# Two attention and mixer layers on one core: where the softmax's small operations stand between VectorE's long products

## The chip, the core and the metric

The kernel runs on one core of a Trainium2 chip. The engines named below are TensorE (PE, matrix products), VectorE (DVE), ScalarE (ACT), GpSimd (POOL) and SyncE (SP, which issues the DMA transfers). The metric is the device time of one execution in microseconds. Before the change it is 1139.48 us, the median of three runs (1139.33 to 1139.99).

## The reference

The input x has 2048 rows of 640 numbers. Two times over, an attention layer and a mixer MLP are added to it:

```
x = x + A(layernorm(x));  x = x + B(layernorm(x));  x = x + A(layernorm(x));  x = x + B(layernorm(x))

A: q, k, v = x @ wqkv            # 640 x 1920, 32 heads of 20 numbers
   row s looks at the rows s, s-2, ..., s-14 (8 keys, those before row 0 masked)
   o = softmax(q.k * 20**-0.5) @ v;   return o @ wo
B: return gelu(x @ w1 + b1) @ w2 + b2      # 640 -> 1536 -> 640
```

Layer norm takes away a row's mean and divides by the root of its variance plus 1e-5. All is float32; the kernel splits each operand of a large product into a float16 and the rest in float16, and adds three products.

## The kernel before

The rows are cut into four units of 512; a unit is four tiles of 128 rows. With two layers there are eight blocks, n = 0 to 7. A block goes through these steps.

- Layer norm "a" (L579 on). A tile's statistics come either from DVE (`FAST` tiles: `bn_stats`, `bn_aggr`, L597 to L599) or from ACT (mean L607, squares L611, variance L621). GpSimd raises variance plus epsilon to the power -0.5: this is "the root", L624 (L602 for a `FAST` tile). ACT then forms a factor (L629), the tile is normalised (ACT L649 or L682, DVE L645), split (ACT L655 or L715 for the high half, L657 or L717 on DVE or POOL for the rest) and transposed by DMA (L659, L720, L725).
- The projection to q, k and v on PE: L913 with evictions L933 in blocks 0 to 3; in blocks 4 to 7 by seven products instead of eight (L841, evictions L850 and L859, sums L873; the layer norm's rows are added up in L688 to L695). The result goes out to memory and is fetched back shifted (L965).
- Attention in four groups of eight heads, 32 groups G in all, on DVE: product q*k (L1007, 128x5120), sum over 20 (L1012), mask (L1016, in the units that begin at row 0), maximum (L1019), difference (L1020), exp on ACT (L1022), sum (L1024), reciprocal (L1025), product (L1026), then the product with v (L1028, 128x5120), and sums over the eight keys (L1033 twice, L1036). ACT L1041 and L1044 (DVE or POOL) split the result; DMA transposes it (L1053).
- The output projection on PE (L1065), in a bank that ACT fills with x first (L1077) and evicts (L1082).
- Layer norm "b", and the MLP: first product L1132 on PE, gelu L1138 and its high half L1141 on ACT, the rest L1143 on DVE or POOL, second product L1153. The weights are split from float32 (ACT L542, L543, DVE or POOL L544), spilled and loaded again (L1125). The MLPs of the last two blocks are computed together at the end (L1293 on).

No loop sets the order in which an engine does its work. Every operation is handed to the class `Plan` (L86) with its engine, its duration, a priority (lower goes first) and its inputs. `Plan.run` plays a clock for each engine, takes the operation that can start first, and writes down the order; the program is emitted in that order, and each engine issues its own instructions in it, one behind the other. So a table such as `ROWS_AT` (the priorities of the layer norms by block) moves instructions on all engines. `wait` is how long DVE is kept for an urgent operation (`PATIENCE` for those below -200), `hold` a time that an operation on DVE is kept back after it could run, for the benefit of POOL. An operation of the kind `either` is done on DVE, or on POOL if it fits beside a reduction L1012.

Operations on DVE that read two operands in the on-chip memory carry `pair=True` (their kinds stand in `PAIRS`). The plan assumes that a root cannot begin while one of them runs. It keeps these stretches in a list `shut`; a root that falls in one is planned at its end. Two such operations that follow each other are one stretch, unless the second is of a kind in `LETS`, or the first was the product with v. This rule is arithmetic in the plan alone: the chip is told of no dependency from a root to DVE's operations.

## Time and profile before

| | |
|---|---|
| profiled execution | 1139.51 us, span 1137.7 us |
| PE busy | 1121.7 us, 99% |
| DVE busy | 1050.8 us, 92%; 25.00 of the 25 us from 600 on, 17.27 of the next 25 |
| ACT busy | 665.4 us, 58%, 20 table loads each at L1022 and L1138 |
| POOL busy | 163.8 us, 14%, of these 69.1 in 31 roots L624 |
| idle of PE ahead of L1065 | 5.6 us in 3 waits, the longest 4.4 us |

A row of the timeline reads: start and duration in us, engine, line, operation, what it writes and reads, how many instructions in a row, and in brackets how long the engine stood idle before it and what ended that. A row of the page's list of groups has after the bar the busy time, the mean of one in ns, and the idle time in front of the group with its releasers. PEld is PE's loading of weights, which runs beside the products. PE's granted clock is given as a share of the full clock. An engine's operation can be recorded as beginning a little before the one ahead of it ends.

### The profile page before, as it was taken

The page shows a single profiled execution, that of the slowest core. Times are in us where ns is not written, and L with a number is a line of the kernel's source. Part 1 is how long each engine was busy: PE and PEld are TensorE (multiplying, and loading weights), DVE is VectorE, ACT ScalarE, POOL GpSimd, SP SyncE. Part 2 cuts the span into 40 slices and gives each one's busy share as a digit, 9 for nine tenths or more (in the row PEclk, how much of TensorE's full clock was granted, in tenths as well). Part 3 has the DMA queues.
Part 4 walks back from the last instruction along what each step waited for, and adds up shares of the span by engine and source line. Part 5 has one row for each costly group of instructions (what it writes and reads, how often), then busy time and mean ns, then how long its engine had stood idle before and what let it go on. Part 6 is the DMA issues. An engine that isn't in the chain of part 4 may idle for free. (4 is left out here: it accounts for less than half of the span.)

```text
span 1137.7 us, 17017 instructions
## 1 busy us (share of the span) xinstructions
PE 1121.7 (99%) x6536; PEld 603.1 (53%) x6536; DVE 1050.8 (92%) x894; ACT 665.4 (58%) x1226; POOL 163.8 (14%) x111
## 2 busy tenths in 40 slices
PE   9999999999999999999999899999999999999998
PEld 6444464445545455455544454456445555654476
DVE  7999999999999999999999799999989998668972
ACT  6468345657856455655745576369744752858630
POOL 1116001201022011210013431003300200000000
PEclk9999999999999999999999999999999999999999
DMA  9999675889898797687786679859698656695201
GB/s 316 299 331 263 204 202 166 296 266 299 258 315 252 199 296 216 204 215 187 288 223 218 141 190 229 307 188 226 150 349 239 184 189 167 175 258 157 68 24 70
DMA packets 262605, 250.91 MB, mean 221 GB/s; under 512 B 154412, under 2 KB 219260, under 8 KB 262524
## 3 DMA queue, kind: packets, MB, share of 16 engines
q1 hardware_dynamic: 262524, 249.83, 75.5%
q8 instruction: 51, 0.84, 0.3%
q14 instruction: 30, 0.25, 0.1%
HBM read 161.49 MB, written 52.64 MB: 188 GB/s over the span
## 5 line engine op out<-in xcount | busy, mean ns | idle before, releaser
L1153 PE MATMUL acc<-c,act 128*128 128x512 f16 (+1 forms) x1728 | 250.9, 299 | 0.5 <-ACT acc L1113 0.3
L1132 PE MATMUL ps<-yT,c 128*128 128x512 f16 x1080 | 246.3, 381 | 3.1 <-issue 2.6
L913 PE MATMUL ps<-wq,yT 128*128 128x480 f16 (+1 forms) x990 | 196.6, 360 | 0.4 <-ACT wq L509 0.4
L1153 PEld LDWEIGHTS <-act 128*128 128x128 f16 x1728 | 136.7, 98 | 112.1 <-issue 0.9
L1028 DVE TENSOR_TENSOR pr<-sm,v 128x5120 f32<-128x5120 f32 x32 | 176.5, 5516 | 0.4
L1007 DVE TENSOR_TENSOR pr<-qk 128x5120 f32<-128x5120 f32 x32 | 175.4, 5481 | 0.2
L1012 DVE TENSOR_REDUCE sm<-pr 128x256 f32<-128x5120 f32 x32 | 175.3, 5478 | 0.2
L1132 PEld LDWEIGHTS <-c 128*128 128x128 f16 x1080 | 103.4, 98 | 126.0 <-issue 5.1
L913 PEld LDWEIGHTS <-yT 128*128 128x128 f16 x990 | 95.4, 98 | 98.5 <-issue 0.5
L1065 PE MATMUL ps<-wo,yT 128*128 128x320 f16 x960 | 134.7, 302 | 5.6 <-ACT ps L1077 5.6
L1033 DVE TENSOR_TENSOR pr<-pr 128x2560 f32<-128x2560 f32 x64 | 137.5, 2148 | 0.1
L624 POOL TENSOR_TENSOR ln<-ln,half 128x2 f32<-128x2 f32 (+1 forms) x31 | 69.1, 2229 | 356.0 <-ACT ln L621 355.9
L1065 PEld LDWEIGHTS <-yT 128*128 128x128 f16 x960 | 94.7, 99 | 45.1 <-issue 5.8
L841 PE MATMUL ps<-wq,yT 128*128 128x480 f16 x528 | 112.2, 366 | 1.1 <-ACT ev L850 1.1
L1138 ACT ACTIVATE act<-ps,b 128x512 f32<-128x512 f32 x72 | 49.2, 683 | 84.0 <-PE ps L1132 83.5
L850 ACT ACTIVATE ev<-ps 128x480 f32<-128x480 f32 x96 | 53.6, 567 | 75.4 <-PE ps L841 72.8
L841 PEld LDWEIGHTS <-yT 128*128 128x128 f16 x528 | 51.1, 98 | 54.9 <-issue 1.5
L841 PE MATMUL ps<-wq 128*128 128x480 f16 x336 | 72.0, 366 | 0.0
L933 ACT ACTIVATE ev<-ps 128x480 f32<-128x480 f32 x64 | 36.1, 566 | 58.6 <-PE ps L913 58.1
L1044 POOL TENSOR_TENSOR ohl<-w,ohl 128x640 f16<-128x640 f32 x18 | 25.2, 1402 | 243.7 <-DVE sm L1024 61.5
L1141 ACT ACTIVATE act<-act 128x512 f16<-128x512 f32 x72 | 44.8, 623 | 22.3 <-PE acc L1153 22.0
L1143 DVE TENSOR_TENSOR act<-act 128x512 f16<-128x512 f32 x64 | 43.6, 685 | 10.6 <-ACT act L1141 10.6
(225 smaller groups left out, 1309.7 us busy)
## 6 DMA issues: line engine op xcount, KB each, us to landing
c<-mw SPq DMA_DIRECT2D x126, 320.0 KB, 3.8
spill<-ev SPq DMA_DIRECT2D x64, 480.0 KB, 4.1
qk<-spill SPq DMA_DIRECT2D x32, 880.0 KB, 5.6
v<-spill SPq DMA_DIRECT2D x32, 880.0 KB, 4.9
qk<-spill SPq DMA_DIRECT2D x32, 320.0 KB, 3.2
c<-in_B_w_dram SPq DMA_DIRECT2D x24, 320.0 KB, 5.2
mw<-c SPq DMA_DIRECT2D x24, 320.0 KB, 4.9
pr<-in_B_w_dram SPq DMA_DIRECT2D x24, 320.0 KB, 4.5
```

What stands on the lines that cost most here:

```text
L624: pool(0.5, prio, lambda t0=t0, t1=t1: nc.gpsimd.tensor_tensor(col(2)[:, t0:t1], col(2)[:, t0:t1], half[:, t0:t1], op=OP.pow), need=[("vr" ...
L841: nc.tensor.matmul(ps, r(x_, j), w[:, j, y_], start=start and i == 0, stop=i == len(todo) - 1, skip_group_check=True)
L850: act(C, -400 + n, lambda: nc.scalar.activation(to(), tile_of(*bank)[:, :C].rearrange("p (a c) -> p a c", a=3), AF.Copy, scale=1.0 / WS), ...
L913: nc.tensor.matmul(ps, transposed(yk)[:, a * KD + k, t * P:(t + 1) * P], wq[:, g, k, b, i0 * GC:i1 * GC], start=first and j == 0, stop=las ...
L1007: nc.vector.tensor_mul(pr.rearrange("p w t c -> p w (t c)"), w[:, HALO + m:HALO + 2 * m].rearrange("p t c -> p (t c)")[:, None, :].to_broa ...
L1012: dve(E, G - 0.7, lambda: nc.vector.tensor_reduce(by_key(), heads(), axis=AX.X, op=OP.add), need=[("qk", G)], give=[("lg", G)], use=[*pk, sk])
L1028: dve(E, G - 0.85, lambda: nc.vector.tensor_mul(heads(), by_key()[:, :, :, None].to_broadcast([P, W, m * GH, DH]), windows(tile_of(*vw), [ ...
L1033: dve(m * w * GC, G - 0.9, lambda w=w: nc.vector.tensor_add(pr[:, 0:w], pr[:, 0:w], pr[:, w:2 * w]), need=[last], give=[("ad", G, w)], use=vk)
L1065: nc.tensor.matmul(tile_of(*pk)[:, :D // 2], transposed(yk)[:, a * KD + k, t * P:(t + 1) * P], wo[:, b, k, c * D // 2:(c + 1) * D // 2], s ...
L1132: nc.tensor.matmul(tile_of(*pk)[:, :nt], tile_of(*ck)[:, a, k * P:(k + 1) * P], transposed(yk)[:, c * KD + k, t0 * P:t1 * P], start=i == 0 ...
L1138: act(nt, -430, lambda pk=pk, h32=h32, e=e: nc.scalar.activation(tile_of(*h32)[:, :nt], tile_of(*pk)[:, :nt], AF.Gelu_apprx_tanh, bias=b1[ ...
L1153: nc.tensor.matmul(accs[k][:, c0:c0 + n], tile_of(*hk)[:, a, (i - t0) * P:(i - t0 + 1) * P], tile_of(*wk)[:, c, w0:w0 + n], start=first, s ...
```

## The change

It alters five things.

1. Of the softmax of group G the priorities go from G - 0.8 to G - 1.96 up to G - 1.92, and the maximum needs the product with v of the group before, so it comes after that.
2. `LETS` and `before` are gone: on DVE, two-operand operations that follow each other always make one stretch in which the plan lets no root begin. A root is planned at 0.6 us instead of 0.5.
3. `FAST` gives two tiles of block 1's layer norm "a" to ACT instead of DVE. (Block 0 keeps its three.)
4. `PATIENCE` goes from 0.6 to 0.1 us; the time at which an operation became ready counts in DVE's choice only where it has a `hold`.
5. Tables of priorities and holds have other numbers.

```
-FAST = {0: (0, 1, 2), 1: (0, 1, 2, 3)}
+FAST = ([0, 1, 2], [0, 1])
...
-HOLD = {'lo': 0, 's': 2, 'hlo': 0, 'b': 0, 'xb': 50, 'ol': 12, 'ol3': 5}
+HOLD = {'lo': 0, 's': 2, 'hlo': 0, 'b': 0, 'xb': 20, 'ol': 12, 'ol3': 0}
...
-ROWS_AT = (-500, -199, -98, -17, -96, -95, -194, -93)
+ROWS_AT = (-500, -199, -198, -17, -16, -15, -94, -13)
...
-    LETS = ("pv", "hlo", "lo", "at", "xb")
-
-    PATIENCE = 0.6
+    PATIENCE = 0.1
...
-                    key = (max(t - o["wait"], clock[e] + 0.05, (o["born"] + o["hold"]) * (e == "dve")), o["prio"], o["n"])
+                    key = (max(t - o["wait"], clock[e] + 0.05, (o["born"] + o["hold"]) * (e == "dve" and o["hold"] > 0)), o["prio"], o["n"])
...
-                    if shut and t - shut[-1][1] < 0.05 and before != "pv" and kind not in self.LETS:
+                    if shut and t - shut[-1][1] < 0.05:
                         shut[-1][1] = t + d
                     else:
                         shut.append([t, t + d])
-                before = kind
...
-            pool(0.5, prio, rstd, need=[("sq", name, t), "half"], give=[("r", name, t)], use=[lk], pair=True)
+            pool(0.6, prio, rstd, need=[("sq", name, t), "half"], give=[("r", name, t)], use=[lk], pair=True)
...
-        dve(L, G - 0.8, lambda: nc.vector.tensor_reduce(mx(0), lg(), axis=AX.X, op=OP.max), need=last, give=[("mx", G)], use=[sk])
-        dve(L, G - 0.8, lambda: nc.vector.tensor_sub(lg(), lg(), mx(0)[:, :, :, None].to_broadcast([P, m, GH, W])),
+        dve(L, G - 1.96, lambda: nc.vector.tensor_reduce(mx(0), lg(), axis=AX.X, op=OP.max),
+            need=[*last, *[("pv", G - 1)] * (G > 0)], give=[("mx", G)], use=[sk])
+        dve(L, G - 1.95, lambda: nc.vector.tensor_sub(lg(), lg(), mx(0)[:, :, :, None].to_broadcast([P, m, GH, W])),
             need=[("mx", G)], give=[("sub", G)], use=[sk])
...
-        dve(L, G - 0.8, lambda: nc.vector.tensor_reduce(mx(1), lg(), axis=AX.X, op=OP.add), need=[("e", G)], give=[("s", G)], use=[sk])
-        dve(8 * m * GH // 2, G - 0.8, lambda: nc.vector.reciprocal(mx(1), mx(1)), need=[("s", G)], give=[("rc", G)], use=[sk])
-        dve(L, G - 0.8, lambda: nc.vector.tensor_mul(lg(), lg(), mx(1)[:, :, :, None].to_broadcast([P, m, GH, W])),
+        dve(L, G - 1.94, lambda: nc.vector.tensor_reduce(mx(1), lg(), axis=AX.X, op=OP.add), need=[("e", G)], give=[("s", G)], use=[sk])
+        dve(8 * m * GH // 2, G - 1.93, lambda: nc.vector.reciprocal(mx(1), mx(1)), need=[("s", G)], give=[("rc", G)], use=[sk])
+        dve(L, G - 1.92, lambda: nc.vector.tensor_mul(lg(), lg(), mx(1)[:, :, :, None].to_broadcast([P, m, GH, W])),
             need=[("rc", G)], give=[("at", G)], use=[sk])
```

The other tables (`QKV_AT`, `INNER_AT`, `HOLD_A`, `PREP_AT`) change in the same way and tell a reader nothing by themselves. After the diff a line of the kernel has a number two or three lower from L599 on: L1007 is L1004 in the new text, L1012 L1009, L1016 L1013, L1019 L1016, L1020 L1018, L1024 L1022, L1028 L1026, L1033 L1031, L1036 L1034, L1044 L1042, L1143 L1141, L657 L654, L544 L541, L621 L618, L629 L626, L682 L679, the exp L1022 L1020, L1138 L1136, L1041 L1039. The text here uses the numbers of the kernel before.

What that does to the order is seen at two places. The first is block 4 (the profile's 612 to 650 us), on DVE, from the product with v of one group on; w_82 and w_86 hold the group's result, sm_87 and sm_88 are the softmax tiles of two groups in turn. Before:

```order
L1028 TENSOR_TENSOR pr<-sm_88,v_68 128x5120
L1019 TENSOR_REDUCE sm_87<-sm_87 128x32
L1033 TENSOR_TENSOR pr<-pr 128x2560
L1143 TENSOR_TENSOR act<-act 128x512
L1033 TENSOR_TENSOR pr<-pr 128x1280
L1143 TENSOR_TENSOR act<-act 128x512
L1036 TENSOR_TENSOR w_82<-pr 128x640
L1020 TENSOR_TENSOR sm_87<-sm_87 128x256
L1007 TENSOR_TENSOR pr<-qk_67 128x5120
L1143 TENSOR_TENSOR act<-act 128x512
```

And in the new order:

```order
L1026 TENSOR_TENSOR pr<-sm_88,v_68 128x5120
L1141 TENSOR_TENSOR act<-act 128x512
L1016 TENSOR_REDUCE sm_87<-sm_87 128x32
L1031 TENSOR_TENSOR pr<-pr 128x2560
L1141 TENSOR_TENSOR act<-act 128x512
L1018 TENSOR_TENSOR sm_87<-sm_87 128x256
L1031 TENSOR_TENSOR pr<-pr 128x1280
L1034 TENSOR_TENSOR w_86<-pr 128x640
L1022 TENSOR_REDUCE sm_87<-sm_87 128x32
L1004 TENSOR_TENSOR pr<-qk_67 128x5120
L1141 TENSOR_TENSOR act<-act 128x512
L1042 TENSOR_TENSOR ohl_75<-w_86,ohl_75 128x4x160
```

The sum over the exps (L1024, now L1022) has moved from behind the next q*k product to ahead of it, and it is an operation with one operand; the difference has moved ahead of the shorter L1033, and an L1044 that POOL did is now DVE's.

On ACT at the same place, before (ln_90 is the layer norm's tile of numbers by row):

```order
L629 ACTIVATE ln_90<-ln_90 128x1 x2
L621 ACTIVATE ln_90<-ln_90 128x2
L682 ACTIVATE w_85<-xf,ln_90 128x640
L682 ACTIVATE w_83<-xf,ln_90 128x640
L1022 ACT_TABLE_LOAD
L1022 ACTIVATE sm_87<-sm_87 128x256
L1138 ACT_TABLE_LOAD
L1138 ACTIVATE act<-ps_94,b_103 128x512
L1041 ACTIVATE ohl_75<-w_82 128x4x160
L1141 ACTIVATE act<-act 128x512
```

And now:

```order
L618 ACTIVATE ln_90<-ln_90 128x2
L1020 ACT_TABLE_LOAD
L1020 ACTIVATE sm_87<-sm_87 128x256
L1136 ACT_TABLE_LOAD
L1136 ACTIVATE act<-ps_93,b_103 128x512
L1039 ACTIVATE ohl_75<-w_86 128x4x160
L1139 ACTIVATE act<-act 128x512
L626 ACTIVATE ln_90<-ln_90 128x1 x4
L679 ACTIVATE w_85<-xf,ln_90 128x640
L679 ACTIVATE w_83<-xf,ln_90 128x640
```

The instructions that wait for the roots (L629, now L626, four in a row instead of two and two) have moved behind the exp, the gelu L1138, L1041 and L1141.

The second place is layer norm "b" of block 1 (300 to 320 us), on DVE; the L657 make the second halves that the transposes carry to PE, c_81 is a piece of MLP weights. Before:

```order
L657 TENSOR_TENSOR w_83<-w_85,w_83 128x640
L1033 TENSOR_TENSOR pr<-pr 128x1280
L1143 TENSOR_TENSOR act<-act 128x512
L544 TENSOR_TENSOR c_80<-c_81,c_80 128x640
L1036 TENSOR_TENSOR w_82<-pr 128x640
L657 TENSOR_TENSOR w_85<-w_86,w_85 128x640
L1026 TENSOR_TENSOR sm_88<-sm_88 128x256
L1007 TENSOR_TENSOR pr<-qk_67 128x5120
```

And now:

```order
L1141 TENSOR_TENSOR act<-act 128x512
L541 TENSOR_TENSOR c_80<-c_81,c_80 128x640
L654 TENSOR_TENSOR w_84<-w_86,w_84 128x640
L654 TENSOR_TENSOR w_85<-w_83,w_85 128x640
L1018 TENSOR_TENSOR sm_88<-sm_88 128x256
L1031 TENSOR_TENSOR pr<-pr 128x1280
L786 SCALAR_TENSOR_TENSOR wq<-wq 128x3x480
L1022 TENSOR_REDUCE sm_88<-sm_88 128x32
L1034 TENSOR_TENSOR w_86<-pr 128x640
L541 TENSOR_TENSOR c_81<-c_79,c_81 128x640
```

The last L657 stands ahead of the shorter L1033 instead of behind it and L1036. The weights' L544 for c_81 stands behind L1036; its input comes from ACT, where an eviction L933, an L787, a table load with the exp, an L542, an L787 and an L543 now follow each other.

14 lines of the change are left out of this document (7 added, 7 removed).

## The prediction

> **What bounds the kernel now.** I began with the page's busy times.
>
> ```profile
> PE 1121.7 (99%) x6536; PEld 603.1 (53%) x6536; DVE 1050.8 (92%) x894; ACT 665.4 (58%) x1226; POOL 163.8 (14%) x111
> ...
> L1132 PE MATMUL ps<-yT,c 128*128 128x512 f16 x1080 | 246.3, 381 | 3.1 <-issue 2.6
> L1065 PE MATMUL ps<-wo,yT 128*128 128x320 f16 x960 | 134.7, 302 | 5.6 <-ACT ps L1077 5.6
> L624 POOL TENSOR_TENSOR ln<-ln,half 128x2 f32<-128x2 f32 (+1 forms) x31 | 69.1, 2229 | 356.0 <-ACT ln L621 355.9
> L841 PE MATMUL ps<-wq,yT 128*128 128x480 f16 x528 | 112.2, 366 | 1.1 <-ACT ev L850 1.1
> ```
>
> TensorE (PE) is busy for 1121.7 of 1137.7 us, and the change leaves its work alone. So no more can be won than what PE loses, and that lies in few places: 5.6 us ahead of the projection (L1065), 3.1 ahead of the first MLP product (L1132), 1.1 ahead of L841. GpSimd's root (L624) has a mean of 2229 ns, much for two numbers a partition. The timeline of the largest loss says why:
>
> ```profile
> 620.17 2.83 DVE L1033 TENSOR_TENSOR pr<-pr 128x2560 f32<-128x2560 f32 x1
> ...
> 620.87 11.76 POOL L624 TENSOR_TENSOR ln<-ln,half 128x2 f32<-128x2 f32 x1 [10.84 <-ACT ln L621]
> ...
> 622.90 0.70 DVE L1143 TENSOR_TENSOR act<-act 128x512 f16<-128x512 f32 x1
> ...
> 623.50 1.50 DVE L1033 TENSOR_TENSOR pr<-pr 128x1280 f32<-128x1280 f32 x1
> ...
> 625.50 0.83 DVE L1036 TENSOR_TENSOR w<-pr 128x640 f32<-128x640 f32 x1
> 626.24 0.43 DVE L1020 TENSOR_TENSOR sm<-sm 128x256 f32<-128x256 f32 x1
> ...
> 626.58 5.50 DVE L1007 TENSOR_TENSOR pr<-qk 128x5120 f32<-128x5120 f32 x1
> ...
> 632.66 0.48 ACT L629 ACTIVATE ln<-ln 128x1 f32<-128x1 f32 x2 [8.73 <-POOL ln L624]
> ...
> 633.31 0.69 POOL L624 TENSOR_TENSOR ln<-ln,half 128x2 f32<-128x2 f32 x1 [0.68 <-ACT ln L621]
> ...
> 639.76 0.69 DVE L1143 TENSOR_TENSOR act<-act 128x512 f16<-128x512 f32 x1 [7.69 <-ACT act L1141]
> ...
> 647.60 0.74 ACT L715 ACTIVATE w<-w 128x640 f16<-128x640 f32 x1 [4.22 <-DVE w L694]
> ...
> 649.97 0.78 ACT L1077 ACTIVATE ps<-xf 128x320 f32<-128x320 f32 x2
> ...
> 650.45 18.97 PE L1065 MATMUL ps<-wo,yT 128*128 128x320 f16 x120 [4.37 <-ACT ps L1077]
> ```
>
> Read it downwards. The root begins at 620.87 and ends only at 632.63, right after the q*k product L1007 (626.58 + 5.50 = 632.08); the next root, at 633.31 with VectorE (DVE) idle, takes 0.69. In between DVE ran operations with two operands in the on-chip memory and nothing else. ScalarE (ACT) stood 8.73 us at L629, with the exp, a gelu, L1041 and L1141 queued behind it. DVE then stood 7.69 us for that L1141, L694 came late, ACT's L715 stood 4.22 us for it with the projection's fills L1077 behind, and PE stood 4.37 us. Nothing on that path is slow in itself; one root was.
>
> ```profile
> 156.57 16.46 PE L1065 MATMUL ps<-wo,yT 128*128 128x320 f16 x120
> ...
> 650.00:675.00 25.00, 24.55 (x149) 15.50 (x149) 24.96 (x14) 20.85 (x49) 4.69 (x4) 0.89 0.86 191
> ```
>
> The same 120 projections take 16.46 us elsewhere and 18.97 here: the second row (a stretch of 25 us with its length, each engine's busy time and count, then the granted clock, the DMA share and GB/s) gives a clock of 0.89, where 1.00 is usual. The loss is thus 4.37 + 18.97 − 16.46 = 6.9 us.
>
> **The change, part by part.** A, *the root at 620.* In the new order a one-operand sum (L1024) stands between L1036 and L1007, with the small maximum and its difference moved about it. The root's longest stretch ahead of that sum is L1033, L1143, the difference, L1033, L1036: 2.83 us, then 0.70, 0.43, 1.50 and 0.83, in sum 6.3, against 11.76; and ACT now issues the exp, the gelu, L1041 and L1141 ahead of L629, so that what is left of the root's time holds none of them. DVE's 7.69 us idle goes with it, so both engines move forward together, and the gain is not merely handed to the next DVE wait. Bounds: nothing, if ACT is held elsewhere; 6.9 if all goes. I take −6.9, because both the root and the order on ACT behind it change. One L1044 moves from POOL to DVE there, an operation of L1036's size (0.83 us), and the transposes that SP issues behind it no longer wait for POOL; what is late next is the root at 673.77 (below).
>
> B, *the gap at 313.*
>
> ```profile
> 310.57 2.31 SPq L659 DMA_TRANSPOSE yT<-w  x1
> ...
> 316.54 11.56 PE L1132 MATMUL ps<-yT,c 128*128 128x512 f16 x45 [2.56 <-issue]
> ...
> 197.17 10.16 PE L1132 MATMUL ps<-yT,c 128*128 128x512 f16 x45
> ```
>
> The releaser reads "issue", but these products need the transposes of the fourth tile, issued only at 310.57, when DVE had come to the L657 ahead of them. Loss: 2.56 + 11.56 − 10.16 = 4.0 us. The new order puts the last two L657 ahead of L1020 and the shorter L1033, so this wait should go. But a second product on PE now meets a new one: it reads weights whose preparation sits, on ACT, behind an eviction, L787, a table load and the exp.
>
> ```profile
> L933 ACT ACTIVATE ev<-ps 128x480 f32<-128x480 f32 x64 | 36.1, 566 | 58.6 <-PE ps L913 58.1
> L1022 ACT ACT_TABLE_LOAD x20 | 25.7, 1283 | 0.4
> L1022 ACT ACTIVATE sm<-sm 128x256 f32<-128x256 f32 x32 | 13.3, 416 | 22.0 <-DVE sm L1020 21.7
> L787 ACT ACTIVATE wq<-wq 128x1440 f16<-128x1440 f32 (+1 forms) x8 | 8.0, 997 | 7.1 <-DVE wq L775 6.0 <-DVE wq L789 1.1
> L542 ACT ACTIVATE c<-c 128x640 f32<-128x640 f32 x24 | 17.3, 726 | 4.1 <-DMA c<-in_B_w_dram 4.1
> L543 ACT ACTIVATE c<-c 128x640 f16<-128x640 f32 x24 | 17.3, 728 | 0.4 <-DVE c L544 0.2
> L544 DVE TENSOR_TENSOR c<-c,c 128x640 f16<-128x640 f32 x21 | 16.9, 820 | 0.5 <-ACT c L543 0.5
> ...
> 304.25 3.42 PE L1153 MATMUL acc<-c,act 128*128 128x512 f16 x24
> ```
>
> From the end of the L913 group: 0.57 + 2 × 1.00 + 1.28 + 0.42 + 0.73 + 0.73 + 0.82 = 6.5 us, while PE has one group of 24 L1153 ahead (3.42). That is 3.1 us of waiting, and up to 1.4 more (11.56 − 10.16) if the clock falls as it did at 316.54; half of that is 0.7. Between −4.0 (no new wait: the modelled starts are off by 3 us) and +0.5 (3.1 + 1.4 − 4.0) I take −4.0 + 3.8 = −0.2, nearest to the rows.
>
> C, *small waits at evictions and fills.* Of the 5.6 us of L1065 1.2 are not the large one, and L841 has 1.1: 2.3 in all. The softmax operations moved forward and the long holds cut (`xb` 50 to 20) leave 2 to 5 us less DVE work ahead of each group, summed over the new order with the rows' means. I take half, −1.2; bounds 0 and −2.3.
>
> D, *two tiles' layernorm to ACT.*
>
> ```profile
> L597 DVE BATCH_NORM_STATS2 bn<-xf 128x6 f32<-128x320 f32 x14 | 6.2, 482 | 2.2 <-DMA xf<-in_A_x_dram 2.2
> L645 DVE TENSOR_SCALAR w<-xf,bn 128x640 f32<-128x640 f32 x7 | 4.2, 608 | 0.8 <-POOL bn L602 0.7
> L607 ACT ACTIVATE junk<-xf 128x640 f16<-128x640 f32 x57 | 41.8, 732 | 5.0 <-DVE xf L1197 3.2 <-DMA xf<-in_A_x_dram 0.7
> L611 ACT ACTIVATE junk<-xf,ln 128x640 f16<-128x640 f32 x57 | 46.6, 818 | 0.4
> L649 ACT ACTIVATE w<-xf,ln 128x640 f32<-128x640 f32 x37 | 32.9, 910 | 3.1 <-DVE w L657 2.0 <-POOL ohl L1044 1.1
> ...
> 0.00:50.00 50.00, 48.23 (x310) 29.29 (x311) 40.88 (x65) 28.82 (x50) 8.01 (x17) 1.00 1.00 309
> ```
>
> DVE loses 2 × (2 × 0.48 + 0.61) = 3.1 us and a few small ones; ACT gains 2 × (0.73 + 0.82 + 0.91) = 4.9 us, and 1.3 for each of two added table loads. ACT is busy for 28.82 of the first 50 us and 58% of the span, so PE's own work covers it: 0. Were the cover gone, those two tiles would come late once, by at most the 4.9 us; POOL's mean load is unchanged (14%).
>
> E, *small new waits.* Nearly every group's order on ACT and DVE changes, and a softmax sum or reciprocal put earlier may find its exp not done (L1024 waits 1.6 us in all now). For three waits of half a microsecond I take +1.5; bounds 0 and 3.
>
> Sum: −6.9 − 0.2 − 1.2 + 0 + 1.5 = −6.8 against the profiled execution's 1139.51 us (its span and 1.8 around it), which is the median 1139.48 but for 0.03: **1132.7 us**.
>
> **A rule against it.** Which operations hold a root back?
>
> ```profile
> 296.55 2.76 DVE L1033 TENSOR_TENSOR pr<-pr 128x2560 f32<-128x2560 f32 x1
> ...
> 298.29 1.57 POOL L624 TENSOR_TENSOR ln<-ln,half 128x2 f32<-128x2 f32 x1 [13.82 <-ACT ln L621]
> ```
>
> Here the root waited for the L1033 it met (to 299.31) and ended at 299.86, though another two-operand operation, an L1143, follows in the order: it got in at the first boundary. At 620.87 it let six such boundaries pass. So a root may enter between two long products, but not surely. The Trainium skill, "SBUF — State Buffer", section "Who interferes with whom", says that a VectorE instruction with two SBUF inputs and a GpSimd instruction that reads SBUF exclude each other for the whole instruction, whichever issues first. By that rule alone a boundary suffices and merging stretches in the plan buys nothing, which is the first rival below; the trace agrees with it at 298.29 (1.57 us) and not at 620.87 (11.76 us).
>
> **The rivals.**
>
> *No change: the hold is not of the kind that the plan now models.* If the root at 620.87 was late for another reason than the unbroken two-operand run, the sum L1024 in between lets nothing in, ACT's new order merely moves L629 behind the gelu, and L682, L715 and L1077 come as late as now. Then A is 0 and the sum 0.1: 1139.6 us. For it: 298.29 shows entries that need no one-operand operation. Against: 632.63 is within 0.6 us of L1007's end, so DVE did hold it, and ACT's queue is shorter either way. Also here belongs a gain at 650 that the next wait takes back: the chain of waits has a root of 5.30 us at 673.77 next.
>
> ```profile
> 673.77 5.30 POOL ln L624
> ```
>
> *Slower: a root held in the longest stretch that the new order leaves.* In blocks 6 and 7, where L1028, the sums L1033 and L1036, L692 to L695 and the next L1007 follow each other, the new order has up to 21.9 us without a one-operand operation (sum of row means). The chip is not told of the plan's rule; a root that becomes ready some microseconds earlier than planned enters that stretch and keeps ACT as at 620, for up to 10.1 us longer than 11.76. PE's wait of 4.37 would grow by as much to 14.5, less 7.4: PE's work ahead of block 7's projection exceeds DVE's by 32.4 us in the new order and by 25.0 at 650 in the old one (orders summed with the rows' means). That leaves 7.1, and with 2.5 for the clock (18.97 − 16.46) 9.6. The sum is −6.8 + 9.6 = +2.8: 1142.3 us. It decides from a hold of some 14 us on. For it: root times of 5.3 us at 673.77 show that holds recur. Against: before has a stretch of 24.6 us too, and no root but one exceeds 6.5 us.
>
> *Better: B's new wait does not come.* The second product's weights are ready in time, and the small waits go too: −6.9 − 4.0 − 2.3 + 0 = −13.2, 1126.3 us. For it: DVE has less work ahead at every group. Against: 6.5 us on ACT behind 3.42 on PE.
>
> **How the numbers follow.** The forecast gets 0.52, no change 0.15, slower 0.19, better 0.14. The forecast's own range is 1129 to 1137 (B and C at their ends). To leave out no more than 2 in 10, the range runs from 1126.5 to 1142.0, which cuts half of the better and of the slower case. A measurement of this kernel tells 0.2% (2.3 us) from no change; that bound runs from 1137.2 to 1141.8. The forecast and the better case are faster (0.66), the second is the same (0.15), the third slower (0.19).
>
> **What would show it.** Right: no L624 above 7 us near 620; L629 not waiting 8 us; DVE's idle before L1143 from 10.6 us down to about 3; the waits of L1065 for L1077 from 5.6 to about 1; no 0.89 clock at 650. B right: no "issue" wait of 2.56 at L1132, and one of some 3 us at L1153 for L544. Wrong: PE's total of waits falls by less than 3 us, a new L624 of over 12 us, or DVE waiting for exps by more than 5 us.

## The result and the profile after

The changed kernel takes **1132.5 us**, the median of four runs (1132.41 to 1133.96). Before took 1139.72 in the four runs beside them (1139.33 to 1139.99). The ratio is 0.994, with a 95% interval from 0.9923 to 0.9957: faster by 0.4 to 0.8%, and 0.2 us from the forecast.

The page of the changed kernel, its busy times and then the groups that answer to those shown of before:

```profile
PE 1118.3 (99%) x6536; PEld 602.0 (53%) x6536; DVE 1050.9 (93%) x885; ACT 672.8 (59%) x1241; POOL 144.6 (13%) x109
...
L1151 PE MATMUL acc<-c,act 128*128 128x512 f16 (+1 forms) x1728 | 250.4, 300 | 3.2 <-ACT c L540 2.8
L1130 PE MATMUL ps<-yT,c 128*128 128x512 f16 x1080 | 243.7, 379 | 0.1
...
L1063 PE MATMUL ps<-wo,yT 128*128 128x320 f16 x960 | 132.0, 299 | 0.0
L838 PE MATMUL ps<-wq,yT 128*128 128x480 f16 x528 | 112.6, 366 | 1.8 <-ACT ps L856 1.8
...
L621 POOL TENSOR_TENSOR ln<-ln,half 128x2 f32<-128x2 f32 (+1 forms) x32 | 52.4, 1638 | 315.2 <-ACT ln L618 315.2
```

DVE is as busy as before (1050.9 against 1050.8 us). PE waits nowhere ahead of the projection (L1063, 5.6 us before), and no longer ahead of the first MLP product (L1130, 3.1 before). In place of the second there is a wait of 2.8 us ahead of the second product, L1151, for the weights that ACT makes in L540. The mean root, now L621, went from 2229 to 1638 ns.

The view of waits of the same kernel, in us, times and the longest:

```profile
DVE sm L1022 <- ACT sm L1020: 4.5, 7, 1.0
...
ACT ln L626 <- POOL ln L621: 3.8, 6, 1.1
PE acc L1151 <- ACT c L540: 2.8, 1, 2.8
PE ps L838 <- ACT ps L856: 1.8, 2, 1.2
...
DVE act L1141 <- ACT act L1139: 0.9, 3, 0.5
```

ACT's wait for roots fell from 19.3 to 3.8 us, and DVE's for L1139 from 10.6 to 0.9. What grew is the wait of the softmax sum for its exp, from 1.6 to 4.5.

The timeline of block 4, where before lost the most:

```profile
621.83 2.82 DVE L1031 TENSOR_TENSOR pr<-pr 128x2560 f32<-128x2560 f32 x1
...
622.00 4.13 POOL L621 TENSOR_TENSOR ln<-ln,half 128x2 f32<-128x2 f32 x2 [11.49 <-ACT ln L618]
...
624.56 0.68 DVE L1141 TENSOR_TENSOR act<-act 128x512 f16<-128x512 f32 x1
...
627.76 0.41 DVE L1022 TENSOR_REDUCE sm<-sm 128x32 f32<-128x256 f32 x1
...
629.08 0.84 ACT L626 ACTIVATE ln<-ln 128x1 f32<-128x1 f32 x4
...
644.33 16.46 PE L1063 MATMUL ps<-wo,yT 128*128 128x320 f16 x120
...
650.00:675.00 25.00, 25.00 (x159) 14.86 (x157) 24.86 (x15) 19.48 (x45) 2.74 (x3) 1.00 0.51 145
```

Both roots together take 4.13 us, where one alone took 11.76, and are over at 626.13, before the sum L1022 that the forecast named begins at 627.76. ACT's L626 waits for nothing, PE goes straight on at 644.33, its 120 products take 16.46 us as elsewhere, and the clock is 1.00.

**Where the 7 us lie.** For every product on PE I took the time to the next one's start, less what a product of its width takes when nothing is in the way (the median of these steps: 216 ns at 512 columns, 202 at 480, 136 at 320). What is left over is PE's loss; waits and half clock are both in it. By stretches of the span, in us:

```
stretch         before   after   difference   term of the forecast
640 to 670        7.00   -0.06        -7.06   A  -6.9
290 to 330        4.91    5.13        +0.22   B  -0.2
all the rest      5.05    4.93        -0.12   C -1.2, D 0, E +1.5
whole            16.96   10.00        -6.96   -6.8
```

The profiled executions differ by 1139.51 - 1132.52 = 6.99 us, so that PE's loss accounts for the whole difference. (With the products of all widths counted, 128 columns too, the whole is 21.1 and 14.2: other sums, the same difference.)

### The profile page after: what moved, and what is told of

It reads as the page before. It is cut to its first block, busy times and chain, and to the rows that moved or that the text cites. A ratio compares the mean times of both kernels' runs of the same rounds, so it can differ in the third digit from the quotient of the medians.

```text
span 1130.7 us, 17031 instructions
## 1 busy us (share of the span) xinstructions
PE 1118.3 (99%) x6536; PEld 602.0 (53%) x6536; DVE 1050.9 (93%) x885; ACT 672.8 (59%) x1241; POOL 144.6 (13%) x109
## 4 chain that ended last, share of the span: by engine, by line
PE 68%; DVE 19%; issue 5%; DMA 4%; SPq 2%; ACT 2%; POOL 0%; DVEq 0%; ACTq 0%; POOLq 0%
PE acc L1151 15%; PE ps L1130 15%; PE ps L910 13%; PE ps L838 10%; PE ps L1063 6%; PE acc L1332 3%; DVE pr L1031 3%; PE ps L1367 3%; DVE pr L1026 3%; DVE pr L1004 3%; DVE sm L1009 2%; PE ps L1332 2%; DMA c<-in_B_w_dram 1%; DVE w L654 1%; DVE act L1141 1%
## 5 line engine op out<-in xcount | busy, mean ns | idle before, releaser
L1151 PE MATMUL acc<-c,act 128*128 128x512 f16 (+1 forms) x1728 | 250.4, 300 | 3.2 <-ACT c L540 2.8
L1130 PE MATMUL ps<-yT,c 128*128 128x512 f16 x1080 | 243.7, 379 | 0.1
L1151 PEld LDWEIGHTS <-act 128*128 128x128 f16 x1728 | 136.8, 98 | 114.7 <-issue 5.3
L1004 DVE TENSOR_TENSOR pr<-qk 128x5120 f32<-128x5120 f32 x32 | 175.1, 5473 | 1.5 <-DMA qk<-spill 1.2
L1026 DVE TENSOR_TENSOR pr<-sm,v 128x5120 f32<-128x5120 f32 x32 | 175.7, 5490 | 0.8
L1009 DVE TENSOR_REDUCE sm<-pr 128x256 f32<-128x5120 f32 x32 | 175.1, 5472 | 0.0
L1130 PEld LDWEIGHTS <-c 128*128 128x128 f16 x1080 | 103.6, 98 | 122.0 <-DVE c L541 0.6
L1031 DVE TENSOR_TENSOR pr<-pr 128x2560 f32<-128x2560 f32 x64 | 137.7, 2151 | 0.1
L1063 PE MATMUL ps<-wo,yT 128*128 128x320 f16 x960 | 132.0, 299 | 0.0
L838 PE MATMUL ps<-wq,yT 128*128 128x480 f16 x528 | 112.6, 366 | 1.8 <-ACT ps L856 1.8
L1063 PEld LDWEIGHTS <-yT 128*128 128x128 f16 x960 | 93.8, 98 | 37.7
L1136 ACT ACTIVATE act<-ps,b 128x512 f32<-128x512 f32 x72 | 49.2, 684 | 83.4 <-PE ps L1130 83.0
L621 POOL TENSOR_TENSOR ln<-ln,half 128x2 f32<-128x2 f32 (+1 forms) x32 | 52.4, 1638 | 315.2 <-ACT ln L618 315.2
L838 PEld LDWEIGHTS <-yT 128*128 128x128 f16 x528 | 51.1, 98 | 55.8 <-issue 2.3
L838 PE MATMUL ps<-wq 128*128 128x480 f16 x336 | 71.8, 366 | 1.1 <-ACT ev L847 1.1
L1042 POOL TENSOR_TENSOR ohl<-w,ohl 128x640 f16<-128x640 f32 x18 | 25.3, 1403 | 296.6 <-DVE sm L1024 56.1
L1139 ACT ACTIVATE act<-act 128x512 f16<-128x512 f32 x72 | 44.8, 622 | 21.2 <-PE acc L1151 20.9
L838 PEld LDWEIGHTS <-wq 128*128 128x128 f16 x336 | 32.6, 98 | 35.7 <-issue 1.5
```

What stands on the lines that cost most here:

```text
L621: pool(0.6, prio, lambda t0=t0, t1=t1: nc.gpsimd.tensor_tensor(col(2)[:, t0:t1], col(2)[:, t0:t1], half[:, t0:t1], op=OP.pow), need=[("vr" ...
L838: nc.tensor.matmul(ps, r(x_, j), w[:, j, y_], start=start and i == 0, stop=i == len(todo) - 1, skip_group_check=True)
L1004: nc.vector.tensor_mul(pr.rearrange("p w t c -> p w (t c)"), w[:, HALO + m:HALO + 2 * m].rearrange("p t c -> p (t c)")[:, None, :].to_broa ...
L1009: dve(E, G - 0.7, lambda: nc.vector.tensor_reduce(by_key(), heads(), axis=AX.X, op=OP.add), need=[("qk", G)], give=[("lg", G)], use=[*pk, sk])
L1026: dve(E, G - 0.85, lambda: nc.vector.tensor_mul(heads(), by_key()[:, :, :, None].to_broadcast([P, W, m * GH, DH]), windows(tile_of(*vw), [ ...
L1031: dve(m * w * GC, G - 0.9, lambda w=w: nc.vector.tensor_add(pr[:, 0:w], pr[:, 0:w], pr[:, w:2 * w]), need=[last], give=[("ad", G, w)], use=vk)
```

## The experiments

Was the one held root the whole of it, and what let it in? Where an experiment edits the order itself, the edit is made in the list that `Plan.run` returns, before the program is emitted; `before(a, b)` moves an operation directly ahead of another, `after(a, b)` directly behind. "mx", "s", "at", "qk" and "pv" are the maximum, the sum over the exps, the product L1026, q*k and the product with v, and ("ad", 19, 2) is the shorter L1033, each with the number of its group. Group 20 is the one at 620 us.

### One exchange of neighbours in the kernel before

```
+    before(spot["dve", ("mx", 20)], spot["dve", ("pv", 19)])
```

One maximum goes ahead of the product with v instead of behind it (the change leaves it behind); no other instruction of the kernel moves.

> The kernel before with two neighbours on DVE exchanged in block 4: the maximum L1019 of group 20 stands ahead of the p*v product L1028 of group 19 instead of behind it. Nothing is added; L1028 and the L1033 that needs its result are now neighbours, so DVE should stop for a moment between them (dependent neighbours show a gap of +0.034 us in the trace, others overlap by 0.08 to 0.097). The root that took 11.76 us begins after that place. Theory 1, of the forecast: only a one-operand operation lets a root in; the stretch from L1033 to L1007 still has none, so the root is held 10 to 12 us and the time stays at 1139.5 (+-1). Theory 2, from the traces: a root gets in at any boundary unless DVE has run long without a gap, so that its operations overlap by 0.094 us or more (here since 556 us); a gap at 619.9 brings the overlap back to 0.085, the root gets in at the next boundary in some 2 us, and the whole loss goes: 1132.6 (1131.5 to 1134).

Measured: 1132.40 us (1131.98 to 1133.79), a ratio of 0.9935 (0.992 to 0.995). Its timeline at the same place:

```profile
614.55 0.41 DVE L1019 TENSOR_REDUCE sm<-sm 128x32 f32<-128x256 f32 x1
614.87 5.48 DVE L1028 TENSOR_TENSOR pr<-sm,v 128x5120 f32<-128x5120 f32 x1
620.38 2.83 DVE L1033 TENSOR_TENSOR pr<-pr 128x2560 f32<-128x2560 f32 x1
...
620.96 2.81 POOL L624 TENSOR_TENSOR ln<-ln,half 128x2 f32<-128x2 f32 x1 [10.83 <-ACT ln L621]
...
623.13 0.68 DVE L1143 TENSOR_TENSOR act<-act 128x512 f16<-128x512 f32 x1
```

The root now ends at 623.77, just behind the first boundary (L1033 to L1143), though ahead of it stand two long two-operand operations instead of one, and none with one operand has come between. PE's loss from 640 to 670 is -0.06 us, in the whole span 9.43. So the held root at 620 is the whole gain of the change: an exchange of two neighbours, without any of the change's five parts and with ACT's old order, gets all of it.

### A stop of DVE nearer to the root

```
+    before(spot["dve", ("at", 19)], spot["dve", ("qk", 20)])
```

In the kernel before DVE runs without a gap from 556 to 632 us. This edit makes it stop at 599.7, for 0.034 us.

> The kernel before with one other pair exchanged, 20 us ahead of the root: the product L1026 of group 19 ahead of the q*k product L1007 of group 20, so that it follows the reciprocal L1025 that it needs, and DVE stops for a moment at 599 us. Between that place and the root nothing else is altered. Theory 1 (one-operand operations): no effect on the root, 1139.5. Theory 2 (overlap grown in a long run without a gap): the overlap begins anew at 0.085 at 599 us; at the rate that it grew from 556 us on (0.085 to 0.091 in 15 us, 0.094 in 22) it stands at 0.088 to 0.093 by 621, between the boundaries that let roots in (up to 0.086) and those that did not (0.094 on). If the root gets in: 1132.7; if it doesn't, 1139.5 and an overlap near 0.094. Either tells where the limit lies.

Measured: 1139.86 us (1139.45 to 1141.83), a ratio of 1.0001 (0.9992 to 1.0011). The timeline:

```profile
620.81 2.81 DVE L1033 TENSOR_TENSOR pr<-pr 128x2560 f32<-128x2560 f32 x1
...
621.50 11.76 POOL L624 TENSOR_TENSOR ln<-ln,half 128x2 f32<-128x2 f32 x1 [10.84 <-ACT ln L621]
...
623.54 0.68 DVE L1143 TENSOR_TENSOR act<-act 128x512 f16<-128x512 f32 x1
...
651.08 18.14 PE L1065 MATMUL ps<-wo,yT 128*128 128x320 f16 x120 [4.38 <-ACT ps L1077]
```

The same 11.76 us, and 4.38 on PE instead of 4.37. (That the 120 products take 18.14 us and not 18.97 is the clock's doing, of which the last section tells.) The stop did change how the records of neighbours on DVE overlap, which had been a suspect: 0.074 to 0.076 us here, 0.094 to 0.097 at this place in the kernel before, and 0.077 to 0.086 where other roots got in. The root missed six boundaries all the same, so the size of the overlap doesn't decide.

### A one-operand operation added in the middle

```
+    order.insert(order.index(spot["dve", ("ad", 19, 2)]), dict(spot["dve", ("mx", 20)]))
```

The maximum of group 20 is done a second time, between the first L1143 and the shorter L1033; its result is the same.

> The kernel before with one small operation more: the maximum L1019 of group 20, one operand, is computed a second time between the first L1143 and the shorter L1033 of the stretch in which the root is held (no dependence on its neighbours, so no gap; DVE 0.41 us longer). Theory 1: it lets the root in, which ends at about 623.9 instead of 632.6, and the loss of 6.9 us goes: 1133. Theory 2 by its letter, boundaries overlapping by 0.095 us shut a root out whatever stands behind them: 1139.5. A version of theory 2 in which DVE does not hold the port in a one-operand operation gives 1133 too. So 1139.5 would say that the planner's rule is wrong, 1133 that a one-operand operation suffices.

Measured: 1132.77 us (1132.20 to 1133.14), a ratio of 0.9935 (0.9918 to 0.9951). The timeline:

```profile
621.97 3.29 POOL L624 TENSOR_TENSOR ln<-ln,half 128x2 f32<-128x2 f32 x1 [10.83 <-ACT ln L621]
...
624.62 0.41 DVE L1019 TENSOR_REDUCE sm<-sm 128x32 f32<-128x256 f32 x1
...
625.94 9.04 POOL L624 TENSOR_TENSOR ln<-ln,half 128x2 f32<-128x2 f32 x1 [0.69 <-ACT ln L621]
...
634.36 0.41 DVE L1024 TENSOR_REDUCE sm<-sm 128x32 f32<-128x256 f32 x1
...
635.02 0.48 ACT L629 ACTIVATE ln<-ln 128x1 f32<-128x1 f32 x2 [2.03 <-POOL ln L624]
```

Here the forecast's idea is seen at work: the root lets L1033 to L1143 pass, and ends at 625.26, 0.23 us behind the end of the added operation (625.03). The *second* root is now held for 9.04 us, through six boundaries and until L1024. That costs nothing: ACT did the exp and the gelu before it came to this root's L629, and waited 2.03 us instead of 8.73. So a hold is dear by what stands behind it on ACT, not by its length.

### The change without the sum in between

```
+    after(spot["dve", ("s", 20)], spot["dve", ("qk", 21)])
```

In the changed kernel the sum L1022, on which the forecast's term A rested, goes back behind the next q*k.

> The changed kernel with the operation put back that the forecast named as the one that lets the root in: the sum over the exps of group 20 stands behind the q*k product of group 21 again, as in the kernel before, and no one-operand operation is left between the longer key sum and that product. Theory 1: the root that now ends at 624.97 is held to the end of the product at some 633, ACT's L626 and what follows come 4 to 5 us later, and 2 to 5 us of the gain go: 1134.5 to 1137.5. Theory 2: the root got in at the first boundary, ahead of the sum's place, with an overlap of 0.084; nothing changes: 1132.5 (+-0.7).

Measured: 1133.16 us (1132.59 to 1133.80), a ratio of 0.994 (0.9925 to 0.9955). The timeline:

```profile
621.91 4.13 POOL L621 TENSOR_TENSOR ln<-ln,half 128x2 f32<-128x2 f32 x2 [11.49 <-ACT ln L618]
...
627.78 5.49 DVE L1004 TENSOR_TENSOR pr<-qk 128x5120 f32<-128x5120 f32 x1
633.19 0.41 DVE L1022 TENSOR_REDUCE sm<-sm 128x32 f32<-128x256 f32 x1
```

The roots take the same 4.13 us without it. The sum was not what let them in.

### Two moves: the exchange, and the gap at 313

```
+    before(spot["dve", ("mx", 20)], spot["dve", ("pv", 19)])
...
+    b = ("b", 1)
+    y, yh, yl, yT = spot["act", ("y", b, 3)], spot["act", ("yh", b, 3)], spot["dve", ("yl", b, 3)], spot["sp", ("yT", b, 3)]
...
+    before(y, hi)
+    before(yh, hi)
+    before(hh, hi)
+    before(yl, hlo)
+    after(yT, max(yl, spot["sp", ("yT", b, 2)], key=order.index))
```

In the last tile of block 1's layer norm "b", ACT's L649 and L655 (y, yh) go ahead of an L543 and an L1141 (hi, hh), DVE's L657 (yl) ahead of an L1143 (hlo), an L544 and an L1036, and SP's transposes (yT) ahead of an L554 and an L534. The L543 thereby comes behind the L1141 too.

This tries to get, on top of the exchange, the 4.0 us that before lost at 313 (term B).

> The kernel before with the one exchange that let the root in (maximum L1019 of group 20 ahead of the p*v product of group 19), and the last tile of block 1's layer norm b moved forward: ACT's L649 and L655 of that tile ahead of an L543 and an L1141, DVE's L657 ahead of an L1143, an L544 and an L1036, SP's transposes ahead of a spill and a load. Theory of the gap at 313 (PE waits for these transposes, issued at 310.57): they are issued at about 309, 1.5 us earlier, PE's wait falls from 2.56-2.98 to about 1.2 us, too short for the clock to fall, so the 1.4 us of half clock go too: 2.9 us less than the exchange alone (1132.4), 1129.5 (1128.5 to 1131). Rival (PE waits for something else there, as the releaser 'issue' leaves open, or the weights of L544, now 1 us later, are missed in its place): 1132 to 1134.

Measured: 1132.27 us (1131.99 to 1132.51), a ratio of 0.9935 (0.992 to 0.995): not told apart from the exchange alone, and in the rival's range. The timeline of PE:

```profile
315.26 9.87 PE L1132 MATMUL ps<-yT,c 128*128 128x512 f16 x45 [1.02 <-issue]
...
332.71 1.30 PE L1153 MATMUL acc<-c,act 128*128 128x512 f16 x8 [1.08 <-DVE xf L1197]
```

The gap, 2.56 us before and 2.82 with the exchange alone, went to 1.02, the clock stayed up, and the 45 products take 9.87 us against 11.56 in both. PE's loss from 290 to 330 is 1.66 instead of the exchange's 5.15. But from 330 to 640 it rose from 2.21 to 5.70, beginning at 332.71 with DVE's L1197. From 330 to 640 DVE is busy for 308.8 of the 310 us, so it leaves PE little to gain there: the wait taken from PE comes back as the next waits for DVE or ACT. The next kernel, in which nothing around 313 is altered but the clock happened to stay up, bears this out: it too has the new losses at 333 (0.66 us) and 377 (0.98).

### A short stop right ahead of the root

```
+            dip.append(lambda: nc.vector.reciprocal(mx(1), mx(0)))
...
+    order.insert(order.index(spot["dve", ("mx", 20)]) + 1, dict(spot["dve", ("mx", 20)], emit=dip[0]))
```

In group 20 a reciprocal of the maximum, into the column that the sum later overwrites, stands directly behind L1019 and ahead of the longer L1033. Nothing is moved. The added operation reads what L1019 writes, so DVE stops for 0.034 us ahead of it. (Lines are one to three higher in this kernel: L1036 is the longer L1033, L1146 is L1143.)

> The kernel before with one operation more, ahead of the root's beginning: between the maximum L1019 of group 20 and the longer L1033 that follows it, a reciprocal of the maximum (its result is overwritten before anyone reads it). It needs the maximum, so DVE stops for 0.034 us between the two; no operation changes its place, and all between L1033 and L1007 is as before. If a short stop of DVE shortly ahead of the running operation is what lets a root in at the next boundary: the root takes 2 to 3 us, and the time is 1132.5 to 1133.5. If it was the maximum's move, or the stop must stand directly ahead of the running operation: the root takes 11 to 12 us, 1139.5 to 1140.5.

Measured: 1132.09 us (1131.83 to 1132.38), a ratio of 0.9931 (0.9914 to 0.9947). The timeline:

```profile
620.10 0.35 DVE L1024 RECIPROCAL sm<-sm 128x32 f32<-128x32 f32 x1
620.37 2.76 DVE L1036 TENSOR_TENSOR pr<-pr 128x2560 f32<-128x2560 f32 x1
...
620.66 3.01 POOL L625 TENSOR_TENSOR ln<-ln,half 128x2 f32<-128x2 f32 x1 [10.83 <-ACT ln L622]
...
623.04 0.68 DVE L1146 TENSOR_TENSOR act<-act 128x512 f16<-128x512 f32 x1
```

The root got in at the first boundary, between the same two operations as in the kernel before, where it did not. Three different one-instruction edits thus give the whole gain: a third of a microsecond of added work on DVE is repaid twentyfold. This one seemed to say that a recent stop of DVE lets a root in. The next run tested that.

### The changed kernel without stops of DVE

```
+    before(dves[q - 2], dves[q - 6])
+    before(dves[q - 1], dves[q - 4])
```

The reciprocal L1023 and the product L1024 of group 19 are taken from the end of the five L1195 and put in among them. DVE now has no stop from 561.5 to 626.8 us.

> The changed kernel with the reciprocal L1025 and the product L1026 of group 19 (in the numbers of before) spread among the five L1197 ahead of them, so that no operation follows directly on one that it needs: DVE's two stops at 614.8 and 615.2 us, ahead of the root at 622, fall away and DVE runs without a stop from 561 us on, as in the kernel before from 556 on. If the stops are what lets the root in at the next boundary, it passes the boundary to L1143 now and waits for the one-operand sum at 627.5: 5.5 to 6.5 us instead of 3.2. ACT comes to L629 at 629 only, so the time stays at 1132.5 (+-1). If not: 3.2 us again and 1132.5.

Measured: 1132.82 us (two runs, 1132.25 and 1133.39), a ratio of 0.9936 (0.9916 to 0.9956). The root at 622.30 got in at the first boundary again, after 62.9 us without a stop. In the same run another root did not, at 483.71. First this run, then the changed kernel, POOL's timeline:

```profile
483.71 5.04 POOL L621 TENSOR_TENSOR ln<-ln,half 128x2 f32<-128x2 f32 x1 [0.69 <-ACT ln L618]
```

```profile
482.98 3.00 POOL L621 TENSOR_TENSOR ln<-ln,half 128x2 f32<-128x2 f32 x1 [1.39 <-ACT ln L618]
```

So a stop isn't needed. And the order of the instructions doesn't decide alone: every engine has the same instructions in the same order in these two kernels up to 612 us. They part at the root before this one, at 480.9: it begins 0.192 us ahead of the end of an L1026 in both, and got in there in the changed kernel (0.75 us) but let this boundary and the next pass here (2.09 us). Neither cost PE anything.

### The parts of the change, taken back or done alone

Three kernels undo one part in the changed kernel and two do one part alone in the kernel before, each time with the tables of priorities that the kernel had:

```
after_without_merge_rule    + LETS = ("pv", "hlo", "lo", "at", "xb") and `before` again, root at 0.5
after_old_softmax_order     - G - 1.96 ... 1.92   + G - 0.8; the maximum doesn't wait for pv
after_old_fast_tiles        - FAST = ([0, 1, 2], [0, 1])   + FAST = ([0, 1, 2], [0, 1, 2, 3])
before_with_merge_rule      - LETS, `before`; root at 0.6
before_with_softmax_order   - G - 0.8   + G - 1.96 ... 1.92, the maximum behind pv
```

> The changed kernel with its second part alone undone: the plan again lets a root begin between two-operand operations of the kinds named in LETS or behind the product with v, and plans it at 0.5 us. All else as changed; the plan's order on all engines differs. If the rule carries the gain, a root is held somewhere for 8 us or more with ACT waiting on it, and 4 to 7 us come back: 1136.5 to 1139.5. If, as the traces show, nearly every root gets in at the next boundary anyway and the loss before was one unlucky place, nothing is held: 1132.5 +-2, the rest being other small waits.

> The changed kernel with its first part alone undone: the softmax's small operations have the priority G - 0.8 again and the maximum no longer needs the product with v of the group before. The merge rule stays, so the plan knows where roots may begin. If the small operations' place carries the gain: 1137 to 1140, with a root held for 8 us or more or, since the plan now knows the long stretches, with roots planned late and ACT waiting some microseconds for them. If the rule or the tables suffice: 1132.5 +-2.

> The changed kernel with its third part alone undone: all four tiles of block 1's layer norm a on DVE again. The forecast put this part at 0 (covered by PE's own work, DVE 3.1 us and ACT 4.9 us): 1132.5 +-1.5, through a shifted order only. If the two tiles on ACT are what the first blocks live on, DVE is 3 to 4 us later from 36 us on and the gaps at 300 and 415 grow: 1134.5 to 1136.

> The kernel before with the second part of the change alone: LETS and its companion gone, so that neighbouring two-operand operations are one stretch in which the plan lets no root begin, and a root planned at 0.6 us; the tables, tiles and softmax priorities of before. If the rule is the gain: 1132 to 1135. If a table of priorities only fits the rules with which it was found, as undoing single parts of the change says (20 to 50 us lost): 1145 to 1185, with the losses at weights (L544) and at the last projection rather than at roots.

> The kernel before with the first part of the change alone: priorities G - 1.96 to G - 1.92 for the softmax's small operations, and the maximum after the product with v of the group before; rules, tiles and tables of before. If the small operations' place is the gain: 1132 to 1135, with no root above 6.5 us. If tables fit only their own rules: 1145 to 1185, whatever the roots do.

Measured, with PE's loss by the same sum as above (before 16.96, after 10.00) and the longest row of roots in POOL's timeline (one to three roots that follow each other):

```
                            us        ratio (95%)              loss   longest row
after_without_merge_rule    1161.37   1.0192 (1.0176, 1.0207)  40.88  5.95
after_old_softmax_order     1183.41   1.0383 (1.0367, 1.0398)  60.19  6.24
after_old_fast_tiles        1151.60   1.0111 (1.0094, 1.0127)  28.67  5.48
before_with_merge_rule      1175.02   1.0306 (1.0267, 1.0345)  56.34  5.23
before_with_softmax_order   1137.21   0.9972 (0.9959, 0.9985)  14.68  6.20
```

The first three expectations missed, by 16 to 43 us; `before_with_merge_rule` came out in the range of its second reading, `before_with_softmax_order` between its two. In none of the five is a root held long. What they lose lies elsewhere, as one row each from the views of waits of the first three shows, with the longest wait last. The changed kernel with the old softmax order:

```profile
PE ps L1063 <- DMA yT<-ohl: 29.3, 1, 29.3
```

The one without the merging rule:

```profile
PE ps L1066 <- DMA yT<-ohl: 10.4, 2, 9.8
```

The one with the old `FAST` tiles:

```profile
PE ps L838 <- ACT ev L847: 6.4, 4, 3.7
```

The longest wait of the first two stands at 986 us ahead of an output projection, whose transposes came late; the third is four waits of L838 for evictions, the longest at 463 us. All three lose at the MLP weights too (L541 or L544, 4.4 to 6.4 us in their longest loss). Each of these kernels has a wholly new order. They say nothing of what a part is worth by itself. That a table of priorities fits only the rules with which it was found would explain them, but is not shown: no table was fitted anew. `before_with_softmax_order` comes nearest to an answer: its loss from 640 to 670 is 0.84 us instead of 7.00, and 3.9 of these 6.2 us are back elsewhere, nearly all of them (3.7) as small losses from 670 on.

## Why the prediction was right

**A, the root at 620: size right, reason wrong.** Forecast -6.9, measured -7.06, at the place and along the chain that was named: L624, L629, L1141, DVE, L694, L715, L1077, PE, and then the clock. Three one-instruction edits of the kernel before, each of which ends this hold and has the change's time within the noise, show that this was the whole gain. The step that failed is the sentence that a one-operand sum, standing between L1036 and L1007, would let the root in. It was in before that sum (626.13 against 627.76), and moving the sum away changed nothing. Nor was ACT's new order needed, since the exchange of neighbours works with the old one; that this order would have softened a hold is only argued from the run with the added operation, where a hold of 9.04 us behind the exp and gelu cost PE nothing.

**What lets a root in at a boundary stays open.** Its rule would have to fit these facts. In the kernel before, waiting roots met 20 boundaries between two two-operand operations and got in at 12; six of the eight misses are one root's, at 620. In the changed kernel it was 16 of 17. No root in these kernels passed by an operation with one operand, of which waiting or running roots met 10 in the kernel before, 3 in the changed one and 14 in the one with the added L1019. The kinds of the neighbours don't decide (L1033 to L1143 went both ways), nor the overlap of their records, nor the time since DVE last stopped (in after 62.9 us, out after 23.9). At 620 it comes out alike from run to run: the times of the kernel before and of the changed one repeat within about 0.2%, which 7 us coming and going would exceed. At 480.9, in kernels that are the same up to there, it did not.

One rival was not tested by itself, the moment at which the root begins, since the edits that let it in at the first boundary moved that as well. The three kernels in which it missed at 620 had it 2.12 to 2.13 us ahead of the first boundary, the end of L1033; where it got in it stood 2.25 (the exchange), 2.46 (the short stop) and 2.65 us (the change) ahead, but also 2.12 in the changed kernel without stops.

The Trainium skill, "SBUF — State Buffer", section "Who interferes with whom", has a VectorE instruction with two SBUF inputs and a GpSimd instruction that reads SBUF exclude each other for the length of an instruction; the 16 of 17 agree with that, the six boundaries at 620 do not. That the plan's new rule moved the root to a better moment by design, and not by luck, can't be shown: its arithmetic (a root gets in only at the end of a merged stretch) isn't what the chip does at 16 of 17. As far as the runs tell, it was luck.

**B: right in both places, the sizes a little small.** Forecast was -4.0 for the wait at L1132 and +3.8 for a new one at L1153, sum -0.2; measured +0.22. The timeline of the changed kernel, at layer norm "b" of block 1:

```profile
306.28 3.42 PE L1151 MATMUL acc<-c,act 128*128 128x512 f16 x24
...
307.28 1.40 ACT L784 ACTIVATE wq<-wq 128x1440 f16<-128x1440 f32 x1
...
308.69 1.28 ACT L1020 ACT_TABLE_LOAD   x1
...
311.74 0.72 ACT L540 ACTIVATE c<-c 128x640 f16<-128x640 f32 x1
...
312.51 0.43 PE L1151 MATMUL acc<-c,act 128*128 128x512 f16 x2 [2.81 <-ACT c L540]
...
313.37 4.78 PE L1151 MATMUL acc<-c,act 128*128 128x512 f16 x22 [0.43 <-DVE c L541]
```

PE waits 2.81 + 0.43 us behind the eviction, the L787 (now L784), the table load and the exp, where 3.1 was forecast. Then most of the 22 products run at half clock: they take 4.78 us, where 24 take 3.42, so about 1.6 us more against the 0.7 that the forecast allowed for it (the half of 1.4). The run with two moves adds what the forecast didn't say: where the gap at L1132 is cut without a new one, nothing is won either, since the following waits for DVE and ACT take it.

**C, D and E: right as a sum (+0.3 forecast, -0.12 measured), not term by term.** Of C, L1065's small waits are gone as a whole (1.2 us to 0.0), not by half; L841's are not, it has 1.8 us now instead of 1.1, for L856, which is of E. Losses over 0.5 us between 330 and 900 us stand at 379, 452, 696 and 801 now, in sum 3.5; before, beside the large one, at 415, 421, 444 and 679, in sum 3.0. D's two tiles cost PE nothing that can be seen: its loss in the first 290 us is 1.23 us, 1.68 before. That the time came within 0.2 us of the forecast is thus in part luck: B was off by +0.42 and this sum by -0.42. The forecast's own range of 1129 to 1137 is not what B and C at their ends give (1127.8 to 1134.6); the measured time lies in both.

**The rivals.** No change: refuted, as A came in full. Its part on boundaries was nearer to the chip than the forecast's, since roots do get in without a one-operand operation. Better: refuted by the 2.81 us at L1151. Slower: no root of the changed kernel takes over 4.21 us, in blocks 6 and 7 as little as elsewhere; the five kernels with other orders have none above 6.3 us either. The forecast looked at one other root of the kernel before (298.29); counted over its whole trace, as above, roots mostly get in at the first boundary they meet, so a hold isn't set by the length of the stretch.

**No version beats the change for certain.** The short stop (1132.09), the two moves (1132.27), the exchange (1132.40) and the change (1132.50) lie within what can be told apart. But the first and the third alter one place in one engine's order, and the change five parts of the planner.

## What to carry to other kernels

When one engine is 99% busy, list its few losses and follow the largest back to a single instruction: here seven microseconds hung on one two-number operation, and exchanging two neighbours was worth as much as a new planning rule with new tables. Test the reason by the smallest edit of the old kernel before building a rule on it; a forecast can have the size and the place right and the reason wrong. And don't judge a scheduler's rule by switching it alone, since its tables of priorities were found with all rules together: parts taken back cost 19 to 51 us here, at places that have nothing to do with the root at 620.

## What the runs showed of the hardware

- A GpSimd operation that reads 128x2 numbers can pass by six boundaries between VectorE operations with two operands in the on-chip memory (11.76 us), while most enter at the first they meet, ending 0.55 us behind it. Which of the two happens is settled by something finer than the order of the instructions: at 620 us it repeated from run to run, by the times, and at 480.9 it went both ways in two kernels that are the same up to there.
- The length of a wait alone doesn't tell whether TensorE's clock is halved after it, nor for how long. In the kernel before, a wait of 4.37 us ahead of L1065 was followed by 6.83 us at half clock (18.97 us for the 120 products, 0.89 in the stretch). In the kernel with the early stop a wait of 4.38 us at the same place was followed by 3.41 us (18.14 us, and 0.93):

```profile
650.00:675.00 25.00, 23.19 (x145) 14.79 (x145) 24.96 (x14) 20.89 (x49) 4.06 (x4) 0.93 0.96 196
```

  Ahead of the first MLP product at 313, 2.56 us (before) and 2.82 (the exchange) were followed by 3.41 us at half clock; 1.02 (two moves) and 2.01 (the added operation) by none, nor the 2.10 of the kernel with the short stop, in PE's timeline and the clock of the stretch:

```profile
315.88 9.87 PE L1135 MATMUL ps<-yT,c 128*128 128x512 f16 x45 [2.10 <-issue]
...
300.00:325.00 25.00, 22.52 (x124) 10.78 (x122) 24.86 (x22) 15.47 (x24) 4.39 (x3) 1.00 1.06 300
```

  Yet the changed kernel with the old softmax order was slowed after a wait of 2.16 us, at 289.7. What these have in common is a grid. Within a run the records of half clock begin whole multiples of 3.413 us apart (before: 317.68 and 648.77, which is 97 of them), and last 3.41 us or a multiple, save for the one that the end of the profile cuts off. On this grid I divided the span of all 14 kernels, behind the first 12 us, into steps. Of the steps at full clock, all 25 in which PE stood idle for 2.06 us or more were followed by half clock, and none of the 4551 with 1.92 or less; of the three between these, one (1.93) was and two (1.94 and 1.97) were not. So it is the idle time within one step that tells, and what a wait of 2 us or a few costs hangs on where it falls on the grid: the 2.10 us above had at most 1.77 in one step, the 2.16 us lay in one step whole.
